# S4D convolution and routed layer: the first eight powers of each channel made in the setup

## The chip, the cores and the metric

The kernel runs on one core of a Trainium2 chip. The metric is the device time of one execution in microseconds (us). The engines are named as the profile names them: PE (matrix products; PEld loads its weights), DVE (vector engine), ACT (scalar engine), POOL (GpSimd) and SP, which issues nearly all transfers from one queue in order.

## The reference

Four layers over x of 2,048 tokens by 512 channels, each with a residual and a layer norm: a state-space convolution, a layer that changes two routed tokens, and both once more with the same parameters. The change touches only the making of the convolution's kernel K:

```python
dt = jnp.exp(log_dt)                                    # one per channel, 512
A = -jnp.exp(log_A_real) + 1j * A_imag                  # 512 channels x 128 states
C = (C_real + 1j * C_imag) * dt[:, None]
P = jnp.exp((A * dt[:, None])[:, :, None] * pos)        # pos = 0 .. 2047
K = 2.0 * jnp.einsum("dn,dnl->dl", C, P).real
y = irfft(rfft(u, 4096) * rfft(K, 4096))[:2048] + u * D_skip
```

So K needs, for each channel and state, the powers 0 to 2047 of one complex number, weighted with C and summed over the 128 states.

## The kernel before, in words

**Powers.** A position is written as 64 i + j. For each channel there are two short rows, a "coarse" one (powers of the 64th power) and a "fine" one (powers of the number itself), 32 entries each, with the states on the 128 partitions. A power is kept as a phase (an integer whose overflow is a full turn, so phases are added) and a decay (a float, multiplied). One matrix product of coarse against fine rows, summed over the states, then gives K.

**Kernel steps.** A step (`KStep`) makes this for 16 channels, so for 32 rows (16 channels, coarse and fine); there are 32 steps, eight for each of the four chunks of 128 channels. In a step `phase_init` (ACT) copies the start column of the phases and column 32, and `phase(k)` (POOL, line L454) doubles the row: 1, 2, 4, 8, 16 columns are added to a step 2^k. `decay_init` (ACT, L459) and `decay(k)` (POOL, L465) do the same for the decays, and `decay(5)` (L467) makes the upper half `ml` of the fine rows. `trig` (ACT, L474 to L476) takes sine and cosine of 33 columns of each row into `sc`; `products` (L482 to L489) multiplies them with the decays, on DVE and, by the table `ON_POOL`, in part on POOL; `contract` (PE, L497) sums over the states and ACT copies the result to `kt` (L499); `spectrum` adds D_skip (DVE, L503) and does a first transform on PE (L507); `turn` transposes it on DVE (L517). `ph`, `mg`, `ml` and `sc` have two buffers each.

**Setup.** `setup(c0, c1, room)` makes seven planes of the phases (`pi`) and of the decays (`pf`): plane 0 the start, plane k the step 2^(k-1). It is run twice: for chunk 0 alone straight into `pi` and `pf` (tiles named `su`), and for chunks 1 to 3 together beside the first kernel steps (`su_w`, `su_w3b`, `su_bigB`), whose planes go to DRAM (`pid`, `prd`, by `put`, L347) and come back half a chunk at a time (`load_params`, L297). The first that needs them is step 8.

**Order.** The kernel steps run as a pipeline, `slot(t)`: DVE adds D_skip for step t-1 and makes the products of step t, ACT takes sines for t+1, starts the phases of t+3 and the decays of t+2, POOL makes phases of t+2 and decays of t+1, PE contracts step t. Other work is set between the slot's pieces by plans of positions (`OPENING` up to slot 5, `CONV1` after): the setup of chunks 1 to 3, the statistics of x and, chunk by chunk, the first convolution (`f1`, `kf`, `load`, `front`, `back`, `fin`, `stats`). From slot 6 to 31 the order on DVE, ACT and POOL is the written one; before that, and on PE and SP, the compiler's scheduler sets it. After slot 32 the kernel's tiles are released and the rest follows: end of the first convolution, routed layer, second convolution, routed layer.

Of the kernel before, what the change touches and what calls it, by code (L numbers as in the profile page):

```python
# [30 lines left out]
# Where each step of the work beside the kernel's pipeline, and of what follows it, stands in program order.  # L31
# [179 lines left out]
def in_order(tc, engines):  # L211
    """Instructions traced in the block keep their order on each of these engines."""
# [12 lines left out]
def build(tc, x, lar, aim, cr, ci, ldt, dsk, wr, wg, wu, wd, d1_h, d1k_h, d4_h, w2_h, w3_h, w3b_h, sm_h, out):  # L225
# [6 lines left out]
    with ctx:  # L232
# [43 lines left out]
        prd = dr.tile([7, 128, D, 2], F32, name="prd", tag="prd")  # L276
        pid = dr.tile([7, 128, D, 2], I32, name="pid", tag="pid")
# [13 lines left out]
        pf = kp.tile([128, 2, 7, 64, 2], F32, name="pf", tag="pf")  # L291
        pi = kp.tile([128, 2, 7, 64, 2], I32, name="pi", tag="pi")
# [31 lines left out]
        def setup(c0, c1, room):  # L324
            """Phases and decays of a state's powers: plane k holds those of step 2^(k-1), as (coarse, fine) pairs."""
# [13 lines left out]
            def fplane(k):  # L339
                return pf[:, :, k] if direct else half(pair(10 + 2 * (k % 2)))  # L340

            def iplane(k):
                return pi[:, :, k] if direct else half(pair(14 + 2 * (k % 3)).bitcast(I32))

            def put(dst, k, v):
                if not direct:
                    nc.sync.dma_start(dst[k, :, ds_, :], v.rearrange("p h e t -> p (h e) t"))  # L347
# [39 lines left out]
            u, iv, gi = im, lr.bitcast(I32), sw.bitcast(I32)  # L387
# [7 lines left out]
            V.tensor_scalar(h, u, 32.0, None, op0=OP.mult)  # L395
            V.tensor_copy(iv, h)
            V.tensor_tensor(h, h, iv, op=OP.subtract)
            V.tensor_scalar(iv, h, 2.0**31, None, op0=OP.mult)
            yield
            for k in range(1, 7):  # L400
                d = iplane(k)
                V.tensor_scalar(d, half(ip), k, None, op0=OP.logical_shift_left)
                put(pid, k, d)
                if k % 2 == 0:
                    yield
# [4 lines left out]
            a0, b0 = fplane(0), iplane(0)  # L410
            V.scalar_tensor_tensor(a0[:, :, :, 0], hv(mx), 2.0, hv(dt), op0=OP.mult, op1=OP.mult)
            G.memset(a0[:, :, :, 1], 1.0)
            put(prd, 0, a0)
            V.tensor_scalar(gi, g1, -(2.0**32), None, op0=OP.mult)
            V.tensor_tensor(iv, iv, gi, op=OP.add)
            for p_ in range(2) if direct else (slice(0, 2),):
                V.tensor_tensor(b0[:, p_, :, 0], hv(iv)[:, p_], hv(iv)[:, p_], op=OP.add)
            G.memset(b0[:, :, :, 1], 0)
            put(pid, 0, b0)
            yield  # L420
            for k in range(1, 7):
                d = fplane(k)
                A.activation(d, half(pb), AF.Identity, bias=onet)  # L423
# [10 lines left out]
        class KStep:  # L434
            """Sixteen channels of the kernel and of its spectrum's first stage, in steps."""
# [10 lines left out]
            def phase_init(self):  # L446
                self.ph = kp.tile([128, 32, 33], I32, name=f"ph{self.u}", tag="ph", bufs=KB)
                A.activation(
                    self.ph.bitcast(I16).rearrange("p d (i h) -> p d i h", h=2)[:, :, 0:33:32, :],
# [306 lines left out]
        def opening():  # L756
            ks[0].phase_init()
            ks[0].decay_init()
            for k in range(3):
                ks[0].decay(k)  # L760
                yield
# [670 lines left out]
```

## Time and profile before

| | |
|---|---|
| median of 3 runs | 697.32 us (696.2 to 698.96) |
| span of the profiled execution, first to last instruction | 695.2 us |
| median less that span | 2.1 us |
| busy: DVE, POOL, PE, ACT | 580.9, 500.4, 485.8, 311.1 us |
| mean granted PE clock | 0.882 |
| products of kernel steps 0, 6, 8, 14, 23 begin on DVE at | 41.6, 117.7, 138.9, 196.8, 293.9 us |
| products of the last kernel step begin at | 379.2 us |

The profiled execution has no time of its own beside its span. In a group's row stand line, engine, operation, tiles (out <- in), shapes and count, then busy us and mean ns of one, then the engine's idle time ahead of these instructions and what ended it. A row of the timeline has start and length in us, and in square brackets the idle time before it. Records of neighbouring POOL instructions overlap by some 0.04 us.

### The profile page before, as it was taken

The numbers are of one execution on the slowest core, as the hardware profiler recorded it, in microseconds if no ns is written. First come the engines' busy times: TensorE is split into PE (matmuls) and PEld (weight loads), VectorE is DVE, ScalarE is ACT, GpSimd is POOL, SyncE is SP. The second block draws the span as 40 slices with busy tenths as digits, with TensorE's granted clock in tenths as the row PEclk, the third lists the DMA queues.
The fourth block names the chain that finished last, engine by engine and source line by source line (L and its number), as shares of the span: only waits on it lengthen the run. The fifth ranks groups of instructions, "written<-read, shape, count | busy, mean of one in ns | idle before, by whom it ended". The sixth has DMA issues, their size and how long they took to land.

```text
span 695.2 us, 14060 instructions
## 1 busy us (share of the span) xinstructions
PE 485.8 (70%) x5300; PEld 360.2 (52%) x5300; DVE 580.9 (84%) x1164; ACT 311.1 (45%) x587; POOL 500.4 (72%) x659
## 2 busy tenths in 40 slices
PE   1012433798988898979789987267799888888336
PEld 1001322577855786648776665034678565656112
DVE  7899998687899999989999964985356799999950
ACT  4445645456753647527473121321511615214272
POOL 4879999999999999987993083260257766757252
PEclk9999775699998989979999998769599899999858
DMA  7961204768410977109460699600813748438436
GB/s 212 225 150 72 90 30 144 262 195 234 118 33 28 218 214 171 53 16 245 117 172 2 184 307 345 164 2 11 178 55 86 154 103 176 145 98 239 108 79 180
DMA packets 51709, 97.64 MB, mean 140 GB/s; under 512 B 4885, under 2 KB 35513, under 8 KB 47161
## 3 DMA queue, kind: packets, MB, share of 16 engines
q1 hardware_dynamic: 51512, 96.72, 51.5%
q8 instruction: 42, 0.69, 0.4%
q14 instruction: 27, 0.21, 0.1%
q0 software_dynamic: 128, 0.02, 0.0%
HBM read 70.23 MB, written 26.48 MB: 139 GB/s over the span
## 4 chain that ended last, share of the span: by engine, by line
DVE 33%; POOL 21%; DMA 16%; PE 14%; issue 8%; SPq 6%; ACT 1%; POOLq 0%; DVEq 0%; ACTq 0%
POOL mg L465 6%; DVE vt L638 6%; POOL ph L454 6%; PE zf L593 4%; DVE g L597 3%; DMA x<-in_x 3%; DVE jn L654 3%; DMA xw<-xs 3%; DVE p L609 3%; SPq L561 3%; DMA kf<-kfd 3%; DMA x<-xs 3%; POOL sc L482 2%; POOL ml L467 2%; DVE p L568 2%
## 5 line engine op out<-in xcount | busy, mean ns | idle before, releaser
L465 POOL TENSOR_TENSOR mg<-mg,pf 128x128 f32<-128x128 f32 (+4 forms) x160 | 108.6, 682 | 5.4 <-ACT pf L423 3.1
L454 POOL TENSOR_TENSOR ph<-ph,pi 128x512 int32<-128x512 int32 (+4 forms) x160 | 112.0, 702 | 0.5
L497 PE MATMUL pk<-sc 128*32 128x64 f32 x2048 | 46.3, 247 | 74.2 <-DVE sc L489 63.5
L618 POOL TENSOR_TENSOR y<-p 64x256 f32<-64x256 f32 x76 | 55.9, 736 | 50.0 <-DVE p L609 35.6
L507 PE MATMUL kq<-kt,d1k 128*64 128x128 f32 x512 | 63.4, 402 | 30.8 <-DVE kt L503 22.5
L593 PE MATMUL zf<-z,d 128*128 128x256 f32 x256 | 80.1, 453 | 5.9 <-DVE g L597 5.1
L497 PEld LDWEIGHTS pk<-sc 128*32 128x32 f32 x2048 | 38.4, 126 | 87.8 <-issue 57.8
L638 DVE STREAM_TRANSPOSE vt<-v 128x512 f32<-128x512 f32 x64 | 69.2, 1098 | 3.3 <-ACT v L626 2.5
L597 DVE STREAM_TRANSPOSE g<-zf 128x512 f32<-128x512 f32 x64 | 65.9, 1051 | 7.0 <-PE zf L593 7.0
L626 ACT ACTIVATE v<-pv 128x512 f32<-128x512 f32 x40 | 23.7, 596 | 97.9 <-PE pv L625 97.9
L593 PEld LDWEIGHTS zf<-z,d 128*128 128x128 f32 x256 | 52.7, 222 | 24.9 <-DVE g L597 11.7
L507 PEld LDWEIGHTS kq<-kt,d1k 128*64 128x64 f32 x512 | 40.1, 159 | 46.7 <-DVE kt L503 25.2
L640 PE MATMUL po<-vt,d 128*64 128x256 f32 x256 | 45.0, 432 | 23.1 <-DVE vt L638 22.6
L619 POOL TENSOR_TENSOR y<-p 64x256 f32<-64x256 f32 x76 | 55.6, 731 | 4.6
L625 PE MATMUL pv<-y,w 128*128 128x128 f32 x320 | 54.8, 302 | 5.0 <-POOL y L619 3.7
L524 PE MATMUL pu<-g,w 128*64 128x128 f32 x640 | 50.2, 298 | 10.2 <-DVE g L1297 3.6
L489 DVE TENSOR_TENSOR sc<-mg,sc 128x1024 f32<-128x1024 f32 x32 | 57.3, 1790 | 0.0
L625 PEld LDWEIGHTS pv<-y,w 128*128 128x128 f32 x320 | 45.1, 201 | 19.6 <-POOL y L619 9.5
L482 POOL TENSOR_TENSOR sc<-mg,sc 128x512 f32<-128x512 f32 x25 | 40.8, 1631 | 12.3 <-ACT sc L476 12.3
L609 DVE TENSOR_TENSOR p<-pu,kf 128x1024 f32<-128x1024 f32 x32 | 38.4, 1209 | 12.8 <-PE pu L524 6.2
L524 PEld LDWEIGHTS pu<-g,w 128*64 128x64 f32 x640 | 38.7, 147 | 18.4 <-DVE p L609 6.2
L579 PE MATMUL pv<-p,w 128*128 128x128 f32 x192 | 40.7, 296 | 7.5 <-DVE p L568 7.1
(344 smaller groups left out, 1175.0 us busy)
## 6 DMA issues: line engine op xcount, KB each, us to landing
kf<-kfd SPq DMA_DIRECT2D x144, 128.0 KB, 4.0
kfd<-kd SPq DMA_DIRECT2D x16, 512.0 KB, 6.8
wd<-in_wd SPq DMA_DIRECT2D x4, 1792.0 KB, 14.0
w<-in_w SPq DMA_DIRECT2D x2, 2048.0 KB, 11.1
x<-in_x SPq DMA_DIRECT2D x8, 512.0 KB
xc<-in_x SPq DMA_DIRECT2D x8, 512.0 KB, 6.0
z<-in_x SPq DMA_DIRECT2D x8, 512.0 KB, 6.4
xs<-xc SPq DMA_DIRECT2D x8, 512.0 KB, 4.3
```

What stands on the lines that cost most here:

```text
L454: G.tensor_tensor(self.ph[:, :, n : 2 * n], self.ph[:, :, 0:n], self.step_of(self.pis, k + 1, n), op=OP.add)
L465: G.tensor_tensor(mg[:, :, n : 2 * n], mg[:, :, 0:n], self.step_of(self.pfs, k + 1, n), op=OP.mult)
L489: V.tensor_tensor(sc[:, :, :, at], m.rearrange("p (o d) i -> p o d i", o=1).to_broadcast([128, 2, 16, 32]), sc[:, :, :, at], op=OP.mult)
L497: T.matmul(pk[32 * g : 32 * g + 32, e, :], t[:, 0:32], t[:, 33:97], start=k == 1, stop=k == 0, tile_position=(0, 32 * g))
L507: T.matmul(self.pq[64 * h : 64 * h + 64, :, 4 * g : 4 * g + 4], d1k[:, 64 * g : 64 * g + 64], kt[:, :, 32 - 32 * h : 64 - 32 * h].rearrang ...
L524: T.matmul(pt[64 * par : 64 * par + 64, ri, q, :], w2[:, k1, 64 * ri : 64 * ri + 64], src[:, k1, :], start=True, stop=True, tile_position= ...
L593: T.matmul(pf[:, 16 * s : 16 * s + 16, :], d1[:, 128 * s : 128 * s + 128], z[:, :, 16 * q : 16 * q + 16], start=True, stop=True)
L597: V.transpose(g[:, :, 16 * q : 16 * q + 16].rearrange("p k e -> p e k"), pf.rearrange("p b e -> p e b"))
L609: V.tensor_tensor(pp, pu.rearrange("p (o r) q e -> p o r (q e)", o=1).to_broadcast([128, 2, 2, 2 * CH]), kf.rearrange("p r (o q) e -> p r ...
L618: E.tensor_tensor(y[0:64, :, par, :], p1[ls, 0], p2[ls, 1], op=OP.subtract)
L625: T.matmul(pv[:, k, :], w3[:, 4 * gi + k, :], y[:, k // 2, k % 2, :], start=True, stop=True)
L638: V.transpose(vt.rearrange("p b e -> p e b"), v[:, :, es].rearrange("p k e -> p e k"))
```

## The change

Eleven planes take the place of seven. Planes 0 to 7 are the first eight powers themselves, planes 8 to 10 the steps 8, 16 and 32. The eight powers are made in the setup on POOL, by a new inner function `first_eight`, in three instructions for a state of phases or decays (from 1 to 2, 2 to 4, 4 to 8 planes); for chunk 0 each of these is done for two halves. The fine phase now starts from minus one half step, and the coarse one from a base that is worked out anew in pairs (`bq`, `bi`), so that column 32 is no longer needed: rows have 32 columns instead of 33, `sc` 96 instead of 97. `phase` and `decay` only double from 8 to 16 and from 16 to 32 columns, `phase_init` and `decay_init` copy eight columns. The planes for chunks 1 to 3 go to DRAM in five transfers for each state (two of four planes, three of one) instead of seven of one plane, and each load brings eleven planes instead of seven. The yields of `slot` are kept in number, so that the plans' positions mean the same. The program also gives 4,096 bytes to the descriptors of the dynamic transfers.

```diff
-        prd = dr.tile([7, 128, D, 2], F32, name="prd", tag="prd")
-        pid = dr.tile([7, 128, D, 2], I32, name="pid", tag="pid")
+        prd = dr.tile([11, 128, D, 2], F32, name="prd", tag="prd")
+        pid = dr.tile([11, 128, D, 2], I32, name="pid", tag="pid")
...
+            def first_eight(t, dt_, steps, op, store):
+                s03, s47 = powers(t, (0, 4), 10, dt_), powers(t, (4, 8), 20, dt_)
+                flat = lambda v: v.rearrange("p e t -> p (e t)")
+                for lo, hi, w, dst in ((0, 1, 0, 1), (0, 2, 1, 2), (0, 4, 2, None)):
+                    m = hi - lo
+                    if direct:
...
+                        for h in range(2):
...
+                            G.tensor_tensor(d_, s03[:, h, lo:hi], st_[:, h].to_broadcast([128, m, n]), op=op)
+                    else:
+                        d_ = s47 if dst is None else s03[:, dst : dst + m]
+                        G.tensor_tensor(d_, s03[:, lo:hi], flat(steps[w]).rearrange("p (o e) -> p o e", o=1).to_broadcast([128, m, 2 * n]), op=op)
+                    if dst == 2:
+                        put(store, (0, 4), s03)
+                put(store, (4, 8), s47)
...
-            for k in range(1, 7):
-                d = iplane(k)
-                V.tensor_scalar(d, half(ip), k, None, op0=OP.logical_shift_left)
-                put(pid, k, d)
...
+            first_eight(pi, I32, isteps, OP.add, pid)
...
             for k in range(1, 7):
-                d = fplane(k)
-                A.activation(d, half(pb), AF.Identity, bias=onet)
-                put(prd, k, d)
+                d = fsteps[k - 1] if k < 4 else pf[:, :, 4 + k] if direct else pair((28, 2, 0)[k - 4])
+                A.activation(d, half(pb) if k > 3 and direct else pb, AF.Identity, bias=onet)
+                if k == 3:
+                    first_eight(pf, F32, fsteps, OP.mult, prd)
+                if k > 3 and not direct:
+                    put(prd, (4 + k, 5 + k), d.rearrange("p e (o t) -> p o (e t)", o=1))
...
             def phase(self, k):
-                n = 1 << k
-                G.tensor_tensor(self.ph[:, :, n : 2 * n], self.ph[:, :, 0:n], self.step_of(self.pis, k + 1, n), op=OP.add)
+                n = 8 << k
+                G.tensor_tensor(self.ph[:, :, n : 2 * n], self.ph[:, :, 0:n], self.step_of(self.pis, k + 8, n), op=OP.add)
...
-                if k < 5:
-                    n = 1 << k
-                    G.tensor_tensor(mg[:, :, n : 2 * n], mg[:, :, 0:n], self.step_of(self.pfs, k + 1, n), op=OP.mult)
+                if k < 2:
+                    n = 8 << k
+                    G.tensor_tensor(mg[:, :, n : 2 * n], mg[:, :, 0:n], self.step_of(self.pfs, k + 8, n), op=OP.mult)
...
-                self.sc = kp.tile([128, 2, 16, 97], F32, name=f"sc{self.u}", tag="sc", bufs=KB)
+                self.sc = kp.tile([128, 2, 16, 96], F32, name=f"sc{self.u}", tag="sc", bufs=KB)
...
-    nc = bacc.Bacc("TRN2", target_bir_lowering=False, num_devices=1)
+    nc = bacc.Bacc("TRN2", target_bir_lowering=False, num_devices=1, dynamic_dma_scratch_size=4096)
```

More of the change, by code (lines that the diff above doesn't have):

```diff
@@ L759, in opening @@
             for k in range(3):
-                ks[0].decay(k)
                 yield
-            for k in range(5):
+            for k in range(2):
                 ks[0].phase(k)
                 yield
+            for k in range(3):
+                yield
             ks[0].trig()
-            for k in range(3, 6):
+            for k in range(3):
                 ks[0].decay(k)
@@ L769, in opening @@
             ks[1].phase_init()
-            for k in range(5):
+            for k in range(2):
                 ks[1].phase(k)
+                yield
+            for k in range(3):
                 yield
```

95 lines of the change are left out of this document (57 added, 38 removed).

## The prediction

> **What bounds the kernel now.** I read the page first, then the busy times by stretch, then the chain in two of these stretches.
>
> ```profile
> span 695.2 us, 14060 instructions
> ...
> PE 485.8 (70%) x5300; PEld 360.2 (52%) x5300; DVE 580.9 (84%) x1164; ACT 311.1 (45%) x587; POOL 500.4 (72%) x659
> ...
> DVE  7899998687899999989999964985356799999950
> POOL 4879999999999999987993083260257766757252
> ```
>
> The reader is to see that POOL is full from the fourth slice to the 17th (52 to 295 us), while DVE has free tenths from the seventh to the eleventh and is full from the 12th on.
>
> ```profile
> 0.00:41.60 41.60, 2.05 (x8) 1.78 (x8) 34.48 (x121) 20.61 (x33) 25.44 (x54) 1.00 0.86 210
> 41.60:117.70 76.10, 24.40 (x472) 19.94 (x472) 72.75 (x106) 40.31 (x64) 75.47 (x75) 0.80 0.28 94
> 117.70:138.90 21.20, 15.28 (x177) 11.59 (x178) 15.66 (x17) 10.36 (x14) 20.88 (x28) 0.58 0.63 223
> 138.90:196.80 57.90, 51.30 (x735) 43.67 (x734) 46.65 (x44) 37.00 (x66) 57.24 (x73) 0.97 0.59 166
> 196.80:293.90 97.10, 84.97 (x1085) 64.58 (x1083) 94.78 (x138) 56.74 (x92) 95.80 (x123) 0.93 0.49 127
> 293.90:389.20 95.30, 82.98 (x1078) 63.86 (x1079) 91.95 (x138) 44.11 (x74) 68.90 (x89) 0.93 0.39 102
> ```
>
> Columns after the length are busy us of PE, PEld, DVE, ACT and POOL, then clock, DMA share and GB/s. I cut at the DVE products (L483) of kernel steps 0, 6, 8, 14 and 23: opening, steps 0-5, 6-7, 8-13, 14-22, 23-31. POOL is full to 196.8 us; after it DVE is, with POOL beside it.
>
> ```profile
> by line: POOL mg L465 31.9%; POOL ph L454 22.4%; POOL sc L482 13.2%; POOL ml L467 11.8%; issue 10.7%; POOL sc L486 9.7%; DVE sc L483 1.2%; POOLq L482 0.1%; POOLq L454 0.0%; POOLq L465 0.0%
> ```
> ```profile
> by line: DVE vt L638 12.1%; DMA kf<-kfd 11.8%; SPq L561 9.9%; issue 9.4%; DVE p L568 6.5%; PE zf L593 6.0%; DVE gk L517 5.0%; DVE sc L486 4.9%; DMA kfd<-kd 4.6%; DVE jn L654 3.8%; PE kq L507 3.7%; PE pv L579 3.7%; DVE g L597 3.6%; DVE xc L6
> ```
>
> The first is the chain from 139 to 197 us, the second from 197 to 300. A shorter POOL is worth its time in the first; in the second POOL is not on the chain at all.
>
> **The change, part by part.** *Taken off POOL:* six short doublings in each of 32 steps (1, 2, 4 powers of 32 columns, phase and decay).
>
> ```profile
> L454 POOL TENSOR_TENSOR ph<-ph,pi 128x512 int32<-128x512 int32 x32 | 41.2, 1286 | 0.1
> ...
> L454 POOL TENSOR_TENSOR ph<-ph,pi 128x256 int32<-128x256 int32 x32 | 23.5, 737 | 0.2
> ...
> L454 POOL TENSOR_TENSOR ph<-ph,pi 128x32 int32<-128x32 int32 x32 | 16.9, 529 | 0.0
> L454 POOL TENSOR_TENSOR ph<-ph,pi 128x64 int32<-128x64 int32 x32 | 15.7, 491 | 0.1
> L465 POOL TENSOR_TENSOR mg<-mg,pf 128x128 f32<-128x128 f32 x32 | 15.7, 490 | 0.2
> L465 POOL TENSOR_TENSOR mg<-mg,pf 128x32 f32<-128x32 f32 x32 | 15.1, 473 | 3.6 <-ACT mg L459 1.8 <-ACT pf L423 1.8
> L454 POOL TENSOR_TENSOR ph<-ph,pi 128x128 int32<-128x128 int32 x32 | 14.9, 467 | 0.2
> L465 POOL TENSOR_TENSOR mg<-mg,pf 128x64 f32<-128x64 f32 x32 | 13.7, 429 | 1.4 <-ACT pf L423 1.4
> ```
>
> That is 529 + 491 + 467 + 473 + 429 + 490 = 2,879 ns a step, 92 us in all. Undisturbed they are cheaper:
>
> ```profile
> 119.25 2.16 POOL L482 TENSOR_TENSOR sc<-mg,sc 128x512 f32<-128x512 f32 x1
> 121.50 1.53 POOL L486 TENSOR_TENSOR sc<-ml,sc 128x512 f32<-128x512 f32 x1
> 122.98 0.27 POOL L454 TENSOR_TENSOR ph<-ph,pi 128x32 int32<-128x32 int32 x1
> ...
> 124.74 0.64 POOL L454 TENSOR_TENSOR ph<-ph,pi 128x256 int32<-128x256 int32 x1
> ```
>
> Six in 124.74 - 122.98 = 1.76 us. In steps 0-5 they are dearer; first and last of six rows there, 20.7 us for 30 instructions:
>
> ```profile
> L465 POOL TENSOR_TENSOR mg<-mg,pf 128x128 f32<-128x128 f32 x5 | 4.3, 852 | 0.1
> ...
> L465 POOL TENSOR_TENSOR mg<-mg,pf 128x32 f32<-128x32 f32 x5 | 2.2, 432 | 0.0
> ```
>
> *Added to POOL:* the same products in the setup, 18 instructions. For the first chunk twelve (four each of 128, 256 and 512 columns): 4 x (0.48 + 0.74 + 1.25) = 10 us by the rows, less without DVE beside them; I take 9. For the other three chunks two passes, phases and decays, of 768, 1,536 and 3,072 columns. Nothing so wide is in the trace; nearest is the product of two full operands:
>
> ```profile
> L482 POOL TENSOR_TENSOR sc<-mg,sc x25: 1177/1723/2197, 37.3 to 373.3; 128x512 f32<-128x512 f32 x25
> ```
>
> At 1.177 us for 512 columns the 5,376 columns of a pass take 12.4 us, at the median 18. I take 12.4, because DVE waits during most of a pass. Two memsets go (0.7 us).
>
> *Where it falls.* Built, the changed kernel has on POOL: pass over the phases, half of step 7's phases, products of step 6, pass over the decays, step 8's phases, step 7's decay, products of step 7, and then step 8's decay. Up to step 6's products (119.25 above) 8 phases and 7 decays lose 45 short instructions: 20.7 us in steps 0-5 and some 15 x 0.45 before, less overlap of neighbouring records, 25 us (13 if all cost as little as undisturbed). So they stand at 119.25 - 25 - 0.7 + 9 + 12.4 - 1 = 114 us; the last 1 is waits that POOL had before 42 us and that are mostly replaced by a wait for the new phase base. DVE's setup work hardly grows in number (the fraction of the new base is worked out in pairs, one shift more at 0.83 us, below): I take 2 us, and it has 76.10 - 72.75 = 3.3 us free.
>
> ```profile
> L402 DVE TENSOR_SCALAR su_w3b<-su_bigB 128x768 int32<-128x768 int32 x6 | 4.9, 832 | 0.0
> ```
>
> Products and memset take POOL to 117.5; the decay pass needs its first plane, which DVE writes behind step 6's products, about 119; it ends at 131.5.
>
> What is late then is step 8, the first whose parameters go through DRAM:
>
> ```profile
> 128.41 0.26 ACT L459 ACTIVATE mg<-pf 128x32 f32<-128x32 f32 x1 [5.30 <-DMA pf<-prd]
> ```
> ```profile
> 128.94 0.22 DVE L503 TENSOR_TENSOR kt<-kt,dskt 128x4 f32<-128x4 f32 x1 [4.17 <-ACT kt L499]
> ```
> ```profile
> 119.79 0.51 SPq L347 DMA_DIRECT2D prd<-su_w3b  x1
> 124.55 4.99 SPq L297 DMA_DIRECT2D pf<-prd  x2
> ```
>
> ACT waits for the load at step 8's decay start; behind it in ACT's fixed order stands the copy `kt` of step 6, and behind that on DVE the products of step 7. So everything hangs on that landing, now at 128.3. Behind the pass SP must write 1,536 KB (planes 4 to 7) and read 704 KB.
>
> ```profile
> w<-in_w SPq DMA_DIRECT2D x2, 2048.0 KB, 11.1
> ...
> prd<-su_w3b SPq DMA_DIRECT2D x7, 384.0 KB, 2.6
> ...
> pf<-prd SPq DMA_DIRECT2D x6, 448.0 KB, 3.7
> ```
>
> Bounds of the write: 2.6 us (as for a quarter of it) and 4 x 2.6 = 10.4; of the load 3.7 and 704/448 x 3.7 = 5.8. Nearest is the 2,048 KB row, where two transfers in flight move 4 MB in about 11 us, 370 KB/us: 1,152 KB more than a plane add 3.1, 256 KB more of load 0.7. I take 6 and 4.4. Landing: 131.5 + 0.6 (issues) + 6 + 4.4 = 142.5, **14 us later**; bounds +10 and +24 (no short instruction dearer than 1.76 us a step; write by bytes). The Trainium skill, "DMA: Bandwidth & Descriptors", section "Anatomy of one DMA", gives 2.0 us and bytes at 436 GB/s; the estimate by it is 5.6 and 3.7, a landing 1 us earlier and a sum of 701. The trace's 2.6 us for 384 KB is near its 2.9.
>
> *Steps 8-13* are where POOL's saving pays: 6 x 2.88 = 17 us off 57.2, so PE's 51.3 and DVE's 46.7 set the pace. The floor is 51.3; with handovers I take 54: **-4** (0 to -6.6).
>
> *Steps 14-31* are DVE's. There only less disturbance helps:
>
> ```profile
> L489 DVE TENSOR_TENSOR sc<-mg,sc x32: 1214/2009/2233, 45.2 to 379.8; 128x1024 f32<-128x1024 f32 x32
> ```
> ```profile
> L568 DVE TENSOR_TENSOR p<-pu,kf x24: 1192/1209/1225, 163.2 to 365.2; 128x1024 f32<-128x1024 f32 x24
> ```
> ```profile
> L489 DVE TENSOR_TENSOR sc<-mg,sc 128x1024 f32<-128x1024 f32 x9 | 15.9, 1767 | 0.0
> ```
> ```profile
> L489 DVE TENSOR_TENSOR sc<-mg,sc 128x1024 f32<-128x1024 f32 x9 | 14.9, 1659 | 0.0
> ```
>
> The same instruction takes 1.21 us alone and 2.0 beside POOL; L568, with an operand in PSUM, is never stretched. The last two rows are steps 14-22 (POOL full) and 23-31 (POOL 72%): with 28% of POOL's time free the mean falls only from 1,767 to 1,659, since the long POOL instructions stay. That is 0.1 us for each of some 2.5 such instructions in 18 steps, 5 us of DVE: **-5** (0 to -12).
>
> *Beside other work:* ACT's two start copies grow eightfold in columns (0.31 and 0.26 us to at most 0.6 each), the three trigonometric passes lose 3%: +0.5 us a step on an engine with 37.0 us in 57.9; uncovered, 9 us over 18 steps. Five later parameter loads carry 704 instead of 448 KB, four steps ahead: nothing, or 1 us each. Tiles of 96 and 32 columns instead of 97 and 33, and the smaller descriptor area for three indirect transfers: no row shows a cost of either; I take none.
>
> *Sum:* +14 - 4 - 5 = +5 us on a span of 695.2; the median 697.32 is 2.1 us above that span, which I leave as it is: **702 us**.
>
> **The rivals.** *The relief wins (faster).* The loss up to step 8 is the low end, 10 us, and the freed interface gives DVE the high end later: 10 - 6.6 - 12 = -9, 689 us. Place: the DVE products of steps 8-31, whose time above the shortest of their form is about 33 us in all (9.3 in steps 8-13, 23.8 after); it decides once over a quarter of that and PE's slack in steps 8-13 return. For it: the slope of L489. Against: the chain after 197 us also runs through transfers and PE. The Trainium skill, "GPSIMD Engine Reference", section "Specifications", says that GpSimd shares its SBUF interfaces with VectorE and contends with instructions that have two SBUF inputs; by that rule, the trace agrees (L489 against L568), and this rival is its price here.
>
> *Little is hidden (much slower).* Long POOL instructions at the median rate (18 us a pass), the write by bytes: +24 - 4 - 5 = +15, 712 us. For it: POOL medians are near 1.7 us. Against: DVE is idle beside the passes.
>
> *The change does not do what it says:* the short instructions are mostly waiting for the interface, and the wait moves to the long ones; then 1.76 us a step go, steps 8-13 still end on PE, steps 14-31 gain nothing: +24 - 4 = +20 at worst. I count it with the former.
>
> *A tie:* loss 11, gain 10.
>
> **How the numbers follow.** Forecast case (+1 to +10) 0.47, of which 0.09 lies under half a per cent; much slower 0.15; tie 0.11; relief 0.27. Half a per cent, 3.5 us, is about what a measurement of this kernel tells from no change. Slower 0.38 + 0.15 = 0.53, same 0.09 + 0.11 = 0.20, faster 0.27. The range takes in both outer cases, 689 to 713; the forecast case alone spans 698 to 707.
>
> **What would show it.** Right: DVE products of step 8 about 14 us after 138.9, an ACT wait of over 8 us for `pf<-prd`, POOL with two instructions near 7 us about 105 and 130 us; POOL idle several us in each of steps 8-13, these under 55 us; L489 near 1.6 us in steps 14-22. Wrong: step 8 under 8 us late (then POOL's short instructions were dearer than I took them), steps 14-31 shorter by over 8 us, or POOL still full after step 8.

## The result and the profile after

The changed kernel takes 727.78 us (median of 4 runs, 724.38 to 730.36) against 697.69 us (696.2 to 698.96) of the kernel before in the same comparison: a ratio of 1.0434, interval 1.0393 to 1.0475. The prediction had the direction, but 702 us and a range that ended at 713. The profiled execution took 724.38 us, 1.9 more than its span, with a mean granted PE clock of 0.875 (0.882 before).

The page of the changed kernel, the lines that answer to those of before:

```profile
span 722.5 us, 13878 instructions
...
PE 481.8 (67%) x5300; PEld 358.0 (50%) x5300; DVE 585.7 (81%) x1165; ACT 328.7 (45%) x587; POOL 444.2 (61%) x483
...
DVE  7699899827768998999999993886446699999960
POOL 4799779848767838576667137433164765758352
```

POOL lost 56 us of work (500.4 before) and is full in only three slices of its row, the third, fourth and seventh; the span is 27.3 us longer all the same. The second view tells where: busy time by stretch, cut at the first product (now L517) of kernel steps 0, 6, 8, 14 and 23 and 10 us after that of step 31; columns as in the prediction.

```profile
0.00:49.10 49.10, 2.05 (x8) 1.78 (x8) 38.62 (x151) 23.13 (x36) 33.96 (x53) 1.00 0.80 196
49.10:130.30 81.20, 25.81 (x472) 20.06 (x472) 76.57 (x71) 37.76 (x57) 70.38 (x48) 0.77 0.14 48
130.30:176.40 46.10, 15.18 (x177) 11.35 (x178) 27.46 (x23) 17.21 (x21) 29.97 (x20) 0.59 0.76 271
176.40:231.90 55.50, 50.89 (x728) 43.81 (x727) 42.81 (x45) 38.74 (x64) 38.99 (x39) 0.94 0.64 174
231.90:327.70 95.80, 83.86 (x1092) 64.75 (x1090) 90.18 (x139) 62.63 (x92) 65.05 (x62) 0.95 0.52 138
327.70:415.70 88.00, 79.41 (x1079) 62.05 (x1080) 85.66 (x139) 47.38 (x74) 49.56 (x45) 0.96 0.44 111
```

Against 41.6, 76.1, 21.2, 57.9, 97.1 and 95.3 us before, the stretches differ by +7.5, +5.1, +24.9, -2.4, -1.3 and -7.3. So steps 8 to 31 gave 11 us back, and everything up to step 8 lost 37.5; what follows step 31 adds 0.8. The stretch between the products of step 6 and step 8 has more than doubled, and DVE and POOL are each idle for more than a third of it.

POOL's timeline there, the two passes (L363: the late branch of `first_eight`):

```profile
110.14 2.20 POOL L363 TENSOR_TENSOR su_w3b<-su_w3b,su_w 128x768 int32<-128x768 int32 x1 [0.59 <-DVE su_w3b L432]
112.42 3.74 POOL L363 TENSOR_TENSOR su_w3b<-su_w3b 128x1536 int32<-128x1536 int32 x1
...
117.69 6.98 POOL L363 TENSOR_TENSOR su_bigB<-su_w3b,su_w 128x3072 int32<-128x3072 int32 x1
...
133.40 5.92 POOL L363 TENSOR_TENSOR su_w3b<-su_w3b,su_w 128x768 f32<-128x768 f32 x2 [3.46 <-DVE su_w3b L449]
139.40 7.26 POOL L363 TENSOR_TENSOR su_bigB<-su_w3b 128x3072 f32<-128x3072 f32 x1
```

And DVE's, beside the first pass and behind the second:

```profile
112.81 4.43 DVE L523 TENSOR_TENSOR sc<-mg,sc 128x1024 f32<-128x1024 f32 x1
...
118.07 7.69 DVE L523 TENSOR_TENSOR sc<-ml,sc 128x1024 f32<-128x1024 f32 x1
...
137.76 10.79 DVE L460 SCALAR_TENSOR_TENSOR su_w<-su_w 128x768 f32<-128x768 f32 x3
165.69 0.42 DVE L537 TENSOR_TENSOR kt<-kt,dskt 128x4 f32<-128x4 f32 x1 [17.15 <-ACT kt L533]
```

The product that takes 1.21 us alone took 7.69 us: it began 0.38 us after POOL's instruction of 6.98 us and ended 1.1 us after it. Beside the second pass three squarings of the decays (L460), which take 0.9 to 1.4 us each in the kernel without passes (e2 below), took 10.79 together. Then DVE stood still for 17 us. What it waited for, on ACT and in SP's queue:

```profile
164.76 0.63 ACT L493 ACTIVATE mg<-pf 128x256 f32<-128x256 f32 x1 [14.38 <-DMA pf<-prd]
165.29 0.37 ACT L533 ACTIVATE kt<-pk 128x256 f32<-128x256 f32 x1
```
```profile
148.53 0.33 SPq L349 DMA_DIRECT2D prd<-su_w  x1
148.96 0.39 SPq L349 DMA_DIRECT2D prd<-su_w3b  x1
150.40 0.32 SPq L349 DMA_DIRECT2D prd<-su_w  x1
150.78 1.27 SPq L349 DMA_DIRECT2D prd<-su_bigB  x1
159.95 1.06 SPq L297 DMA_DIRECT2D pf<-prd  x2
```

This is the wait that the prediction named, `kt` of step 6 behind the copy of step 8's first decays, only longer. The pass ended at 139.40 + 7.26 = 146.66; its last write was issued at 150.78, behind three others; the load could follow at 159.95 and landed at 164.76.

### The profile page after: what moved, and what is told of

It reads as the page before. It is cut to its first block, busy times and chain, and to the rows that moved or that the text cites. A ratio compares the mean times of both kernels' runs of the same rounds, so it can differ in the third digit from the quotient of the medians.

```text
span 722.5 us, 13878 instructions
## 1 busy us (share of the span) xinstructions
PE 481.8 (67%) x5300; PEld 358.0 (50%) x5300; DVE 585.7 (81%) x1165; ACT 328.7 (45%) x587; POOL 444.2 (61%) x483
## 4 chain that ended last, share of the span: by engine, by line
DVE 43%; PE 23%; DMA 18%; issue 8%; ACT 4%; SPq 3%; POOL 0%; POOLq 0%; DVEq 0%; ACTq 0%
DVE vt L672 6%; PE zf L627 4%; DVE g L631 4%; DMA kfd<-kd 4%; PE pv L613 4%; DMA x<-in_x 3%; DVE sc L523 3%; DVE p L643 3%; DMA kf<-kfd 3%; DMA x<-xs 3%; PE kq L541 3%; DVE jn L688 2%; PE kx L567 2%; DVE stt L687 2%; DMA xc<-in_x 2%
## 5 line engine op out<-in xcount | busy, mean ns | idle before, releaser
L499 POOL TENSOR_TENSOR mg<-mg,pf 128x256 f32<-128x256 f32 (+1 forms) x64 | 61.6, 964 | 26.8 <-ACT mg L493 26.7
L488 POOL TENSOR_TENSOR ph<-ph,pi 128x256 int32<-128x256 int32 (+1 forms) x64 | 59.2, 927 | 25.0 <-ACT ph L482 24.9
L516 POOL TENSOR_TENSOR sc<-mg,sc 128x512 f32<-128x512 f32 x25 | 40.7, 1628 | 40.0 <-ACT sc L510 40.0
L674 PE MATMUL po<-vt,d 128*64 128x256 f32 x256 | 42.3, 406 | 25.8 <-DVE vt L672 25.1
L653 POOL TENSOR_TENSOR y<-p 64x256 f32<-64x256 f32 x76 | 55.5, 730 | 4.6
L523 DVE TENSOR_TENSOR sc<-mg,sc 128x1024 f32<-128x1024 f32 x32 | 55.9, 1748 | 0.0
L643 DVE TENSOR_TENSOR p<-pu,kf 128x1024 f32<-128x1024 f32 x32 | 38.5, 1212 | 12.2 <-PE pu L558 5.7
L493 ACT ACTIVATE mg<-pf 128x256 f32<-128x256 f32 x32 | 20.5, 645 | 58.9 <-DVE sc L523 44.6
```

Source lines behind the costliest of these rows:

```text
L488: G.tensor_tensor(self.ph[:, :, n : 2 * n], self.ph[:, :, 0:n], self.step_of(self.pis, k + 8, n), op=OP.add)
L499: G.tensor_tensor(mg[:, :, n : 2 * n], mg[:, :, 0:n], self.step_of(self.pfs, k + 8, n), op=OP.mult)
L523: V.tensor_tensor(sc[:, :, :, at], m.rearrange("p (o d) i -> p o d i", o=1).to_broadcast([128, 2, 16, 32]), sc[:, :, :, at], op=OP.mult)
L643: V.tensor_tensor(pp, pu.rearrange("p (o r) q e -> p o r (q e)", o=1).to_broadcast([128, 2, 2, 2 * CH]), kf.rearrange("p r (o q) e -> p r ...
```

## The experiments

All in one table. "Step n" is the start in us of the first product that DVE makes alone in that step (L483 before, L517 after), from one profiled execution each; the ratio is that of the times to those of the kernel before in the same comparison, with its interval. The comparisons were made at different times, and the spans of the kernel before in them range from 689.7 to 700.1 us, so a difference of a few us in a span alone says little.

| kernel | step 0 | step 6 | step 7 | step 8 | step 31 | span | ratio |
|---|---|---|---|---|---|---|---|
| before | 41.6 | 117.7 | 129.1 | 138.9 | 379.2 | 695.2 | 1 |
| after | 49.1 | 130.3 | 166.0 | 176.4 | 405.7 | 722.5 | 1.0434 (1.0393 to 1.0475) |
| e1_split | 48.5 | 124.2 | 160.9 | 171.3 | 403.9 | 718.1 | 1.0346 (1.0265 to 1.0427) |
| e2_no_pass | 48.6 | 126.3 | 155.0 | 165.3 | 397.9 | 715.7 | 1.0248 (1.0170 to 1.0326) |
| e3_chunks | 49.0 | 127.5 | 157.1 | 167.5 | 398.4 | 716.1 | 1.0289 (1.0210 to 1.0369) |
| e4_load | 48.5 | 122.5 | 136.8 | 147.3 | 381.7 | 700.2 | 1.0067 (1.0042 to 1.0091) |
| e7_own | 48.6 | 134.1 | 168.6 | 178.9 | 411.7 | 729.9 | 1.0486 (1.0447 to 1.0524) |
| e8_volume | 48.9 | 122.1 | 148.0 | 158.5 | 394.7 | 712.9 | 1.0234 (1.0197 to 1.0270) |
| e13_volume2 | 48.8 | 122.0 | 142.3 | 154.0 | 394.5 | 716.0 | 1.0232 (1.0202 to 1.0263) |
| e9_mixed | 39.0 | 118.9 | 137.6 | 146.9 | 383.1 | 698.6 | 1.0075 (1.0049 to 1.0101) |
| e10_late | 39.0 | 118.9 | 130.8 | 144.1 | 378.9 | 699.9 | 1.0020 (1.0002 to 1.0038) |
| e11_late_slots | 38.9 | 118.7 | 130.3 | 144.8 | 379.8 | 694.9 | 1.0014 (0.9993 to 1.0035) |
| e14_first12 | 38.9 | 118.8 | 127.9 | 137.7 | 378.7 | 698.7 | 1.0011 (0.9989 to 1.0033) |
| e12_after_late | 50.2 | 131.8 | 153.8 | 172.2 | 407.6 | 725.1 | 1.0371 (1.0331 to 1.0411) |

### The passes: cut, left out, by chunk

**e1_split.** POOL's passes in pieces of 384 columns.

```diff
-                        G.tensor_tensor(d_, s03[:, lo:hi], flat(steps[w]).rearrange("p (o e) -> p o e", o=1).to_broadcast([128, m, 2 * n]), op=op)
+                        for j in range(m):
+                            for s in range(0, 2 * n, 384):
+                                G.tensor_tensor(d_[:, j, s : s + 384], s03[:, lo + j, s : s + 384], flat(steps[w])[:, s : s + 384], op=op)
```

> The changed kernel with each pass of the setup for chunks 1 to 3 cut into POOL instructions of 384 columns (14 in place of 3); the same products, transfers and copies. Theory H (a POOL instruction with two operands holds the interface it shares with DVE until it ends, so a long one stops DVE's two-operand instructions for its whole length): no DVE product of steps 5 and 6 over 3 us (7.69 and 4.43 before the cut), step 6 begins at 120 to 124 us instead of 130, the squarings of the decays are no longer stopped, step 8's decays land some 10 us earlier than 164.8, and the time is 712 to 718 us. Rival W (it is the amount of POOL work and of transfers, the length of one instruction does not matter): 14 instructions cost at least what 3 do, landing at 163 to 168 us, 726 to 733 us.

720.47 us, between the two ranges; step 8 comes 5.1 us earlier than in the changed kernel. No DVE product of steps 5 and 6 takes over 2.2 us any more, as H expected, but POOL's pieces are longer in sum (15.6 us for the 13.2 of the decays' pass). So H names a part of the loss and not the main one.

**e2_no_pass.** The passes of chunks 1 to 3 replaced by DVE copies of the planes, so that planes 1 to 7 of these chunks hold no powers.

```diff
-                        G.tensor_tensor(d_, s03[:, lo:hi], flat(steps[w]).rearrange("p (o e) -> p o e", o=1).to_broadcast([128, m, 2 * n]), op=op)
+                        V.tensor_copy(d_, s03[:, lo:hi])
```

> The changed kernel with the two passes for chunks 1 to 3 left out: DVE copies the planes instead, so the powers 1 to 7 of these chunks are not made (all equal power 0). Everything else stays, the transfers too. It measures what the passes cost together, by length and by amount: theory H and rival W both expect the landing back at 135 to 142 us and a time of 692 to 702 us. If the time stays above 710, neither holds and the transfers (eleven planes, five writes for each state) or the later steps are to blame.

715.09 us, where both theories had 692 to 702. Without any pass on POOL step 8 is still 26.5 us late: the passes carry 11 of the 37.5 us, less what DVE's copies cost in their place (7.6 us of DVE's time). DVE and SP in this kernel:

```profile
128.61 0.55 DVE L449 SCALAR_TENSOR_TENSOR su_w3b<-su_w,dtb 128x384 f32<-128x384 f32 x1
...
133.30 1.76 DVE L363 COPY su_bigB<-su_w3b 128x3072 f32<-128x3072 f32 x1
154.64 0.42 DVE L537 TENSOR_TENSOR kt<-kt,dskt 128x4 f32<-128x4 f32 x1 [19.58 <-ACT kt L533]
```
```profile
137.22 3.85 SPq L349 DMA_DIRECT2D prd<-su_bigB  x1
148.56 1.04 SPq L297 DMA_DIRECT2D pf<-prd  x2
```

L449 is the decays' first value. It runs at 128.6 us although what it needs is there early (in the kernel before its like runs at 66.7), and 3 MB of decays follow it: 11.3 us from the last write's issue to the load's.

**e3_chunks.** Pieces of 256 and 512 columns, a chunk at a time, each chunk's planes written at once (512 KB a transfer).

```diff
+                for q in range(c1 - c0):
+                    e = slice(2 * CH * q, 2 * CH * q + 2 * CH)
...
+                        for j in range(0, m, 2):
+                            i = min(m, j + 2)
+                            G.tensor_tensor(d_[:, j:i], s03[:, lo + j : lo + i, e], flat(steps[w])[:, e].rearrange("p (o e) -> p o e", o=1).to_broadcast([128, i - j, 2 * CH]), op=op)
+                    es = slice((c0 + q) * CH, (c0 + q) * CH + CH)
+                    for k0, v in ((0, s03), (4, s47)):
+                        nc.sync.dma_start(store[k0 : k0 + 4, :, es, :].rearrange("k p e t -> p k (e t)"), v[:, :, e])
```

> As the cut kernel, but each pass goes chunk by chunk in instructions of 256 and 512 columns, and each chunk's planes 0 to 3 and 4 to 7 are written to DRAM by transfers of their own, so that step 8's load waits only for chunk 1. Theory H with the landing as the limit: DVE products as short as in the cut kernel, the last write ahead of the load 512 KB instead of 1,536 KB, landing 5 us earlier than there, 706 to 713 us. Rival W: as the changed kernel less the shorter write, 720 to 726 us.

717.29 us, again between the ranges; step 8 at 167.5, 3.8 us earlier than in e1. Writing by the chunk helps, and is not the answer either.

### Does one long POOL instruction keep DVE out?

Both kernels are the kernel before with 2,048 columns of POOL work more in slots 11, 15, 19, 23 and 27; e5_hold1 as shown, e6_hold8 with two planes of 128 columns an instruction.

```diff
+            if t % 4 == 3 and 10 <= t < 28:
+                for j in range(0, 16, 16):
+                    G.tensor_tensor(spare[:, j : j + 16], w2[:, j : j + 16], ones.rearrange("p (o e) -> p o e", o=1).to_broadcast([128, 16, 128]), op=OP.mult)
```

> The kernel before, with one Pool multiplication of 2,048 columns more in each of the slots 11, 15, 19, 23 and 27, whose result nobody reads. Theory H (a Pool instruction with two inputs keeps DVE's two-input instructions out until it ends): Pool's instruction takes 4 to 6 us, and in these slots a DVE product of 1,024 columns takes 4 us or more, where the longest in the kernel before is 2.2. Theory W (DVE and Pool share word by word): no DVE product over 2.6 us, but several of 2 us beside it.

> The same columns in eight Pool instructions of 256. Theory H: no DVE product over 2.6 us, and Pool's eight take longer in sum than the one, since DVE gets a turn between them. Theory W: the same products as with one instruction, within 0.3 us.

Each ran in a single execution. e5_hold1, POOL's instruction in its first two slots and DVE's work beside them:

```profile
179.73 4.97 POOL L749 TENSOR_TENSOR spare<-w,ones 128x2048 bf16<-128x2048 f32 x1
...
223.43 4.53 POOL L749 TENSOR_TENSOR spare<-w,ones 128x2048 bf16<-128x2048 f32 x1
```
```profile
180.24 5.54 DVE L490 TENSOR_TENSOR sc<-mg,sc 128x1024 f32<-128x1024 f32 x1
...
223.60 0.41 DVE L648 TENSOR_TENSOR xc<-xc,po 128x256 f32<-128x256 f32 x1
223.92 1.06 DVE L598 STREAM_TRANSPOSE g<-zf 128x512 f32<-128x512 f32 x1
225.93 1.06 DVE L598 STREAM_TRANSPOSE g<-zf 128x512 f32<-128x512 f32 x1 [0.95 <-PE zf L594]
226.85 1.14 DVE L504 TENSOR_TENSOR kt<-kt,dskt 128x4 f32<-128x4 f32 x1
```

In the first slot the product waits to the end of POOL's instruction (184.70) and then does its 1.1 us. In the second slot transposes, and an addition with one operand in PSUM (`po`), run at their usual speed beside POOL; the first instruction with two operands in SBUF, `kt`, is held to 227.99, POOL's end at 227.96. In the other three slots it was a product of 1,024 columns (5.52 us), one of 512 (4.98) and an instruction of 128 columns (`jn`, 4.42 us, its like 0.3 right after). The group of products L490 in both kernels, shortest, median and longest in ns:

```profile
L490 DVE TENSOR_TENSOR sc<-mg,sc x17: 1210/2074/5544, 180.2 to 375.0; 128x1024 f32<-128x1024 f32 x17
```
```profile
L490 DVE TENSOR_TENSOR sc<-mg,sc x18: 1282/1752/2083, 180.3 to 377.3; 128x1024 f32<-128x1024 f32 x18
```

With eight pieces none of these is over 2.1 us, as H expected, and POOL's part grows instead; its eight in slot 11 of e6_hold8:

```profile
179.76 7.98 POOL L749 TENSOR_TENSOR spare<-w,ones 128x256 bf16<-128x256 f32 x8
```

H holds: 7.98 us for 4.97. But the times differ by little, 723.96 and 720.77 us, against a median of 698.97 for the kernel before in the same comparison: in one piece a slot POOL's additional work was 24.5 us and the kernel 25.0 us longer, in eight it was 36.6 us and the kernel 21.8 longer.

### Late writing

**e4_load.** The first eight powers of chunks 1 to 3 are made after the load, half a chunk at a time; DRAM holds seven planes again.

```diff
+        def eight(h, which):
+            for t, op in which:
+                v = t[:, h].rearrange("p k e t -> p k (e t)")
+                for lo, hi, w, dst in ((0, 1, 5, 1), (0, 2, 6, 2), (0, 3, 7, 4), (3, 4, 7, 7)):
+                    m = hi - lo
+                    G.tensor_tensor(v[:, dst : dst + m], v[:, lo:hi], v[:, w : w + 1].to_broadcast([128, m, 128]), op=op)
...
-                    put(prd, (4 + k, 5 + k), d.rearrange("p e (o t) -> p o (e t)", o=1))
+                    put(prd, k, flat(d))
```

> Chunk 0 stays as in the changed kernel. For chunks 1 to 3 seven planes are written to DRAM as in the kernel before (384 KB each, in scratch of their own), and the first eight powers of a half chunk are made on Pool after its load, with instructions of 128 to 384 columns. Theory T (the loss before step 8 is the late writing: the passes, 3 MB through DRAM, and decays that wait for scratch that the phases hold): the first products of step 8 come at 142 to 148 us (138.9 before, 176.4 after), and the kernel takes 688 to 700 us. Theory S (the loss sits in what chunk 0 and the steps themselves do now, the copies of eight powers on ACT among them): step 8 at 160 us or later and 710 to 718 us.

Step 8 at 147.3 us, within T's 142 to 148; S falls. The time, 703.89 us, is 4 above T's range: 8.5 us of the delay remain. The decays' first value ran at 67.92 us, and four of the seven phase planes were issued to DRAM from 65 to 77 us, since a plane that holds a step does not need the start value. In the changed kernel planes 1 to 7 are products with the start value, so all eight wait for what is ready last.

**e8_volume and e13_volume2.** e4_load with as many bytes through DRAM as the changed kernel; in e13 (the last two lines) the 2 MB loads of other matrices are kept behind the loads of the planes. The planes of `pid` are doubled likewise.

```diff
-                for a, b, k in ((0, 1, 0), (5, 11, 1)):
+                for a, b, k in ((0, 1, 0), (5, 11, 1), (1, 5, 7)):
...
                     put(prd, k, flat(d))
+                    if k > 2:
+                        put(prd, k + 4, flat(d))
...
-                    with tc.issue_after(ld.ins):
+                    with tc.issue_after(ld[0].ins), tc.issue_after(ld[1].ins):
```

> The kernel of e4_load, which writes four planes of each kind twice and loads them too, so that as much goes through DRAM as in the changed kernel (11 planes); what they hold is not used. If the volume of the transfers is what delays step 8: its first products come 5 to 10 us after those of e4_load (147.3), at 152 to 157 us, and the kernel takes 708 to 715 us. If the transfers are hidden as long as they start early: within 2 us of 147.3, 702 to 706 us.

> The kernel of e8_volume, in which the 2 MB loads of the inverse's matrices are issued behind both loads of step 12's phases and decays; in e8_volume one of them stood ahead of the phases' load (127.48 and 128.02 us in SP's queue). If part of the 11.2 us of e8_volume came from that order: step 8 at 151 to 156 us (147.3 in e4_load, 158.5 in e8_volume), and the difference to 147.3 is the price of the volume alone. If the volume alone made it: step 8 within 1.5 us of 158.5.

713.09 and 714.64 us; step 8 at 158.5 (152 to 157 expected) and 154.0, 11.2 and 6.7 us after e4_load. So the order explains 4.5 us of the first at step 8, as expected, but it is not gained: step 10 begins at 176.0 in e8 and 176.8 in e13 (164.8 in e4_load), and both have the same ratio. In e13 the wait has moved to ACT's copy of a spectrum that waits for a write to DRAM (its timeline):

```profile
175.42 0.60 ACT L577 ACTIVATE kd<-kx 128x512 f32<-128x512 f32 x1 [7.09 <-DMA kfd<-kd]
```

In the whole time the volume costs 11 to 12 us in either order (ratios 1.0234 and 1.0232 for 1.0067); at step 8 it costs 7 to 11.

**e7_own.** The changed kernel, the decays' first value and two of their steps in scratch of their own.

```diff
+        own = kp.tile([128, 3, 384, 2], F32, name="own", tag="own")
...
-            fsteps = [pair(i) for i in (2, 0, 18)]
+            fsteps = [pair(i) for i in (2, 0, 18)] if direct else [own[:, 1], own[:, 2], pair(2)]
```

> The changed kernel, in which the late decays' first value and their first two steps have scratch of their own (9 KB a partition) in place of scratch that the phases' pass and its writes hold. Theory T (decays are made late because they wait for the phases' scratch): L449's answer runs before 110 us instead of at 132.67, the decays' pass starts by 127 us instead of 133.4, the first products of step 8 come at 162 to 170 us (176.4 in the changed kernel), and the kernel takes 714 to 722 us. If the shared scratch is not what holds them (rival: DVE's and ACT's order does): step 8 within 2 us of 176.4 and 725 to 730 us.

The first value moved to 66.70 us: it had been held by the scratch that it shares with the phases. The pass did not follow, and the kernel took 730.6 us. DVE, SP and POOL:

```profile
118.76 7.02 DVE L454 TENSOR_SCALAR su_w<-su_bigB 128x768 int32<-128x768 int32 x1
```
```profile
125.81 0.32 SPq L351 DMA_DIRECT2D pid<-su_w  x1
126.17 3.60 SPq L351 DMA_DIRECT2D pid<-su_w3b  x2
```
```profile
112.71 4.01 POOL L371 TENSOR_TENSOR su_w3b<-su_w3b 128x1536 int32<-128x1536 int32 x1
...
132.31 4.11 POOL L367 TENSOR_TENSOR su_w3b<-own 128x768 f32<-128x768 f32 x2 [3.40 <-DMA pid<-su_w3b]
```

The next holder is the scratch of planes 1 to 3: POOL waits until the phases in it are written. That write was ready when POOL had made plane 3 (112.71 + 4.01 = 116.72), but stood in SP's queue behind plane 9 (`pid<-su_w`), which a DVE instruction made that was held by the pass to 125.78. The instruction with that plane, a shift, has only one operand in SBUF and a number; its like takes 0.55 us at 128.86, and it takes 7.02, from 1.1 us after the start of a POOL instruction (117.71, 7.64 us) to 0.4 us after its end. So the hold is not limited to DVE instructions with two operands, and one unshared place gives nothing; freeing all of the scratch was not tried.

### Chunk 0, and the order on ACT

**e9_mixed.** e4_load, with chunk 0's steps doubling from the first column.

```diff
+            def doubling(self, k):
+                return k - 3 if not self.c else k if k < 2 else None
...
-                n = 8 << k
+                k = self.doubling(k)
+                if k is None:
+                    return
+                n = 1 << k + 3
```

> The kernel of e4_load, with chunk 0 as in the kernel before: its steps double from the first column (five instructions a kind on Pool), and nothing of its first eight powers is made in the setup. Theory T: the first products of step 0 come at 41 to 43 us (49.1 in the changed kernel), those of step 8 at 139 to 143 us, and steps 8 to 31 keep what e4_load gave there (6 us): 694 to 700 us. Rival: step 0's lateness is made good anyway and the delay at step 6 comes from elsewhere: step 6 at 121 us or later, 702 to 705 us.

Step 0 at 39.0 us and step 5 at 102.8 (106.0 before), better than expected; step 8 at 146.9, against 147.3 in e4_load: not 139 to 143. The time is 700.79 us, 0.8 above theory T's range. What e4_load loses by step 0 (48.5 against 39.0 us here) is all made good again before step 8: there the load sets the pace, and it does not hang on chunk 0. For the changed kernel itself this was not tried.

**e10_late, e11_late_slots, e12_after_late.** `decay_init` of step 8 behind `kt` of step 6, in e9_mixed, with four scratch places besides (e11), and in the changed kernel (e12, which has no `eight`).

```diff
-            at(t + 2, "decay_init")
+            if t != 6:
+                at(t + 2, "decay_init")
...
                     at(t, "contract")
+                    if t == 6:
+                        eight(0, EIGHT[1:])
+                        at(8, "decay_init")
```

> The kernel of e9_mixed, in which ACT copies step 8's first decays behind the kernel tile kt of step 6 and not ahead of it, and Pool makes their eight powers there too. Theory K (in e9_mixed the products of step 7 are late because kt of step 6 stands behind a copy that waits for the load): step 7 at 126 to 131 us (137.6 in e9_mixed), step 8 at 139 to 142 us (146.9), the kernel 692 to 697 us. Rival (the load and Pool's powers set step 8, whoever waits): step 8 within 2 us of 146.9 and 699 to 702 us.

> The kernel of e10_late with four places in the scratch for the late decays' planes in place of two, so that ACT does not wait for a plane's write before it makes the next but one (2.74 us in e9_mixed). If that wait is on the way to the load: the load of the decays is issued 2 to 4 us earlier than in e10_late, step 8 comes 1 to 4 us earlier, and the kernel takes 690 to 696 us; if not, all within 1 us of e10_late.

> The changed kernel with the same exchange on ACT alone. Theory K as in the prediction (a long wait of ACT for step 8's decays holds kt of step 6): step 7 at 145 to 156 us (166.0 in the changed kernel), step 8 at 169 to 174 us (176.4), the kernel 720 to 726 us. Rival (the landing of the decays alone counts): step 8 within 1.5 us of 176.4 and 726 to 729 us.

ACT in e10_late:

```profile
126.66 0.36 ACT L520 ACTIVATE kt<-pk 128x256 f32<-128x256 f32 x1
136.25 0.64 ACT L477 ACTIVATE mg<-pf 128x256 f32<-128x256 f32 x1 [9.23 <-POOL pf L308]
```

`kt` no longer waits, and step 7 comes 6.8 us earlier than in e9_mixed, as theory K had it; step 8 only 2.8 us earlier, because the load, POOL's eight powers and the copy follow each other. The time fell to 698.81 us (ratio 1.0020 for 1.0075). In e11 the load was issued at 124.78 instead of 127.10, and nothing followed from it. In the changed kernel (e12) step 7 came 12.2 and step 8 4.1 us earlier, both as theory K had it, and the time was 724.85 us, 2.9 less, which the two intervals don't separate.

**e14_first12.** e11, with steps 8 to 11 doubling from the first column too.

```diff
-                return k - 3 if not self.c else k if k < 2 else None
+                return k - 3 if self.u < 12 else k if k < 2 else None
...
-                        eight(0, EIGHT[1:])
```

> The kernel of e11_late_slots, in which steps 8 to 11 double from the first column too, so that nothing is made on Pool between the first load and step 8. If the powers made after the load are what keeps step 8 at 144 to 145 us: step 8 at 138 to 141 us, and the kernel 692 to 697 us, faster than the kernel before by 0.2 to 0.8%. Rival (the longer copies and what steps 8 to 11 now lose take it back): step 12 within 1.5 us of that of e11_late_slots (182.4) and the kernel within 2 us of it.

Step 8 at 137.7 us: the 5 to 6 us that stayed in e10 and e11 were the powers made after the load. Step 12, at 181.7, is 0.7 us before that of e11, and the time is the same, 698.97 us: the rival was right, and the lead was lost in steps 8 to 11. None of these kernels is faster than the one before.

## Why the prediction was wrong

- **POOL's work removed and added: right.** -92 + 9 + 2 x 12.4 = -58 us was predicted, 500.4 - 444.2 = 56.2 was found. The passes cost 2.20 + 3.74 + 6.98 = 12.9 and 5.92 + 7.26 = 13.2 us, for 12.4.
- **"Up to step 6's products ... 114 us": wrong, 126.6 (L516).** The prices held: the 45 short instructions were 26.3 us of records ("25"), the chunk-0 products cost 9.8 for 9, the phases' pass 12.9 for 12.4. Busy and idle time up to these products, before and after:

```profile
0.00:119.25 119.25, 27.89 (x494) 23.09 (x496) 108.78 (x226) 60.92 (x97) 102.39 (x130) 0.87 0.48 133
```
```profile
0.00:126.63 126.63, 24.70 (x429) 19.49 (x433) 113.71 (x217) 60.43 (x90) 101.03 (x97) 0.86 0.38 100
```

POOL's busy time (the fifth of the pairs) fell by 1.4 us where the sum has 4.3, and its waits grew from 16.9 to 25.6, where the sum lets them fall by 1 ("the last 1 is waits"): 9.7 of the 12.6 us are that term. The time between the products of steps 0 and 5, ahead of the pass, shows why:

```profile
41.59:106.05 64.46, 20.44 (x392) 16.67 (x392) 61.66 (x96) 33.64 (x55) 63.90 (x66) 0.86 0.26 83
```
```profile
49.08:109.98 60.90, 19.61 (x364) 15.27 (x366) 58.47 (x61) 32.42 (x49) 50.68 (x40) 0.84 0.07 17
```

POOL had 13.2 us less to do, DVE 3.2, and the stretch became 3.6 shorter: DVE was 96% busy before and after, and POOL now waits, 5.4 us of it for copies of decays on ACT, which waited 17.3 us for DVE's products. The prediction's own row has DVE at 72.75 us of 76.10 there, and still takes POOL's whole saving off the clock.
- **"I take 12.4, because DVE waits during most of a pass": the reverse.** DVE waited because of the pass: 4.43 and 7.69 us for two products of 1.21. e5 and e6 show the hold by itself. What it is worth: cutting the passes brought step 8 forward by 5.1 us (e1, with longer passes), leaving them out by 11 (e2, with copies on DVE).
- **"It ends at 131.5": 146.66.** The decays' pass started at 133.40 for 119, since its first plane waited for step 6's products as predicted, and these were late. It stands behind them at all because of scratch that the phases hold (e7), which the prediction did not look at. From step 6's POOL products to its end it is 20.0 us for 17.5.
- **Write and load, 0.6 + 6 + 4.4 = 11 us: 18.1.** From 146.66 to 164.76. The last write was issued 4.1 us after the pass: ahead of it in SP's queue stood a plane that ACT made only at 149.46, since the squaring on DVE that it needs (L460) was held by the pass; from its issue to the load's 9.2 us, and 4.8 for the load. The upper bounds were 10.4 and 5.8; the queue before the write had no term. The estimate by the Trainium skill's "DMA: Bandwidth & Descriptors", section "Anatomy of one DMA", was 5.6 and 3.7 us for the two; the section states its figures for transfers issued from GpSimd, and these are issued from SP. With three other writes issued in the 2.3 us before, the trace shows 9.2 and 4.8 and does not agree.
- **The landing, and what hangs on it: right in kind.** ACT's wait is 14.38 us ("over 8"), `kt` stands behind it, and DVE behind that; e12 takes `kt` out and step 7 comes 12.2 us earlier. Landing at 164.76 for 142.5: 22.3 us, which are the 12.6 up to step 6's products, 2.5 from there to the end of the pass and 7.1 from write to landing.
- **Steps 8 to 13, -4: -2.4. Steps 14 to 31, -5: -8.6.** Together -11.0 for -9, right in size. POOL is idle for 16.5 of 55.5 us in steps 8 to 13, as said, though they last 55.5 us and not under 55. Steps 14 to 31 are shorter by more than 8 us, which the prediction had named as a sign against itself. The reason given, less disturbance of L489 (now L523), was right, but not for the rows it was read from: those on `mg` have a mean of 1.82 us in steps 14 to 22 ("near 1.6"), for 1.77 before, and 1.50 in steps 23 to 31, for 1.66, together 1.0 us less; those on `ml`, six in all, take 1.21 us for 2.08 and 1.88, together 4.6 us less. Nor is the gain a fixed one. From step 8 to 31 the table gives 11.0 us for the changed kernel, 7.5 to 9.4 for e1, e2, e3 and e7, 4.1 to 5.9 for e4, e8 to e12, and none for e13 and e14 (where steps 8 to 11 are of the old form). What sets it was not settled.

```profile
L523 DVE TENSOR_TENSOR sc<-mg,sc 128x1024 f32<-128x1024 f32 x9 | 16.3, 1816 | 0.0
L523 DVE TENSOR_TENSOR sc<-ml,sc 128x1024 f32<-128x1024 f32 x3 | 3.6, 1214 | 0.0
```
```profile
L523 DVE TENSOR_TENSOR sc<-mg,sc 128x1024 f32<-128x1024 f32 x9 | 13.5, 1503 | 0.0
L523 DVE TENSOR_TENSOR sc<-ml,sc 128x1024 f32<-128x1024 f32 x3 | 3.6, 1213 | 0.0
```

The rows on `ml` of the kernel before, steps 14 to 22 and 23 to 31:

```profile
L489 DVE TENSOR_TENSOR sc<-ml,sc 128x1024 f32<-128x1024 f32 x3 | 6.2, 2077 | 0.0
```
```profile
L489 DVE TENSOR_TENSOR sc<-ml,sc 128x1024 f32<-128x1024 f32 x3 | 5.6, 1875 | 0.0
```

- **The rival that was nearest** was "little is hidden", 712 us: late writes and slow passes together. It had the upper bounds of both and not DVE's hold, the scratch or the queue. Its +24 is also less than the terms named for that bound give: short instructions at 1.76 us a step put the decays' pass 10.5 us later, the write and load by bytes add 5.8, and with the 14 that is some 30.

So the step that failed is "Where it falls", the clock of POOL up to the landing: 14 us were to be lost up to step 8, 37.5 were. It let POOL's waits shrink by 1 us where DVE was as full and they grew by 8.7, took the passes to be free for DVE, and had no term for the scratch and the queue. Of the 37.5 us the passes carry 11.0 (e2 against the changed kernel). From e2 to e4_load go another 18.0, for planes that are written late: 7 to 11 of them by the volume (e13 and e8), the rest by the late start of the decays, which e7 shows to hang on scratch and queue but does not price. The 8.5 left in e4_load are in part its own, since it makes its powers after the load. That e4_load wins back 29 of the 37.5 us is measured; the split of the 18.0 is worked out from kernels that differ in more than one thing, and stays open.

## What to carry to other kernels

Work taken off an engine moves the end only where that engine is on the chain; where another one is as full (72.75 and 75.47 of 76.10 us here), there is little credit until both are shorter: 13.2 us less on POOL and 3.2 less on DVE gave 3.6. When products are made earlier and kept, ask which operand comes last: here one plane in seven hung on the start value before and eight of eleven after, so that transfers of which some can run from 65 us on (e4_load) fell into the one gap that the next load waits for. A long POOL instruction is to be counted as DVE time wherever DVE's next instruction has two operands in SBUF, and at least for the shift of e7 with one operand too.

## What was not expected of the hardware

- A POOL instruction with two SBUF operands kept such DVE instructions out for its whole length, not in turns: 1.21 us became 7.69 beside one of 6.98 (changed kernel) and 5.54 beside one of 4.97 (e5). A shift with one SBUF operand was kept out in the same way, 0.55 us becoming 7.02 beside one of 7.64 (e7), while transposes (1.06 us) and an addition with a PSUM operand (0.41) ran through. Between two POOL instructions DVE gets its turn (e6: no product of that group over 2.1 us). The Trainium skill, "SBUF — State Buffer", section "SBUF: two separate sides", states just this, an exclusive lock for the whole instruction in place of shared bandwidth; the traces of the changed kernel and of e5 agree, and the prediction, which counted on a slowdown, missed it.
- POOL work added to the kernel before cost about its own length, 25.0 us for 24.5 (e5), also in slots where DVE and not POOL stood on the chain: between steps 14 and 31 four such instructions made 18.8 us. 69 us of short instructions taken out of steps 8 to 31 (24 x 2.88) gave 11. Adding and removing are not mirror images.
